# Two places in VectorE's instruction order and the form of one small addition, in an attention and two-stage expert kernel

## The chip, the cores and the metric

The kernel runs on one core of a Trainium2 chip. The metric is device time in microseconds (us) of one execution. The engines are named as in the profile: PE (TensorE, the matrix engine; PEld is its weight load), DVE (VectorE), ACT (ScalarE), POOL (GpSimd) and SP (SyncE, which issues most DMAs). Each engine runs its own instructions strictly in the order in which the program issues them, and waits for other engines through semaphores.

## The reference

Three parts are computed one after the other.

```python
# 1. a linear recurrence per batch (4) and head (8), 768 steps, head size 48
S = a_t * S + k_t v_t^T          # a_t complex, magnitude clipped at 0.999
y_t = q_t Re(S)
x = y as 3072 rows of 384
# 2. experts, stage one: 8 experts, each row goes to the one with the largest logit
e = argmax(x @ w_gate);  g = softmax(...)[e]
x1 = g * (relu(x @ w1[e]) @ w2[e])        # 384 -> 1024 -> 384
# 3. the same again on x1, with 8 other experts and a bias on the logits
#    that one of two modality labels of the row selects
```

## The kernel before, in words

The recurrence is done in 12 units of 2 x 128 time steps, as matrix products on PE with elementwise work on DVE, ACT and POOL. Each step of a unit has a name and a place in a table (`AT`), and the places are sorted into one written-out order for all engines.

Rows are sorted by expert into tiles of 128 rows, padded so that a tile holds rows of one expert. The sorting is prepared while the recurrence still runs. `Router.batch` takes the logits of `n` blocks of 128 rows, makes the one-hot choice `oh` on DVE, and ranks each row within its expert with a few small matmuls on PE into the PSUM tile `pr` (L470 to L473). The last of these reads `acc`, a 128 x 8 bf16 tile with the counts so far. Then DVE sums the choices of this batch into `su` (L475, 128 x 8 f32), adds them to `acc` (L476), and reads `pr` (L478). In the recurrence `pr` lies in a PSUM buffer that later transposes of the recurrence (L339) use again. There are five such batches for stage one (tile `r1acc`) and six for stage two (`r2acc`), the latter during the tiles of stage one.

Each expert stage runs over its tiles in `Stage.run`. A tile's work is a set of named steps, each with a place between about -2 and 10 in the table `POS[stage]`, and `Stage.tile` sorts them by place. For the four quarters q of the hidden layer the steps are: `g1_q` (18 matmuls on PE, L825 to L827), `hh_q` (ACT, relu to f16, L829), `hl_q` (DVE, the remainder that f16 leaves out, L830), and `g2_q` (6 matmuls on PE, L836 to L838, of which the third reads `hl_q`). Other steps prepare coming rows: `sq` (ACT, L775) and `sv` (DVE, four instructions, L777 to L780) scale the rows of tile j+2, and `T`, `xh`, `xl` transpose those of tile j+1 (L790, L794, L796). `ev` (DVE, L842) and `yo` (ACT, L845, and a scatter by POOL, L846) end a tile. In stage one `sv` stands at 6.511 and `ev` at 7.217.

Weights come in f32 and are split into two f16 parts, in eight pieces: `W.split` does the high part `hmq` on ACT (L748) and the low part `lmq` on DVE (L749), with m=0 for the first layer and 1 for the second and q the quarter. These steps stand in `CHG[stage]` with places from 1 to 13.5; a place of 10 or more means the next tile. Each is inside a branch (L861) that is taken when the next tile has another expert. Several tiles of stage one do it; in stage two the changes of expert are at other tiles, among them the last but one. `LATE` gives other places for the tiles from number 23 on, in both stages.

Steps from outside a stage are put in by the table `EXT`: 26.94 means place 6.94 in tile 2. `gate1` is the last part of stage one's gate weights (its fourth step is the DVE instructions L555 to L564).

## Time and profile before

| what | value |
|---|---|
| time, median of 3 runs (lowest to highest) | 782.65 us (781.81 to 783.91) |
| the profiled execution: its own time, and the span of its instructions | 784.11 us, 782.4 us |
| busy share of the span: PE, PEld, DVE, ACT, POOL | 93%, 75%, 68%, 60%, 37% |
| mean granted clock of PE, of full speed | 0.981 |

The recurrence takes roughly the first 270 us, stage one of the experts goes on to about 556 us, and stage two to the end. All rows below are of the profiled execution; its time lies 1.5 us above the median, so a difference worked out in it is taken to the median.

### The profile page before, as it was taken

Reading aid. Unit: us, or ns where it says so; the run is one execution under the profiler, and the core shown is the slowest. Engines: PE = TensorE matmul, PEld = TensorE weight load, DVE = VectorE, ACT = ScalarE, POOL = GpSimd, SP = SyncE. Lnnn points to the kernel's source line nnn. Section 1 sums busy time; section 2 is a strip of 40 time slices with the busy share of each in tenths; the row PEclk is TensorE's granted clock in tenths of the full one; section 3 lists DMA queues with packets and bytes.
Section 4 is the critical chain, followed back from the end, with each engine's and each line's share of the span. In section 5 each row is a group of like instructions: output and inputs, shape, how many; then the busy total and the mean of one; then the engine's idle time right before and its main releaser. Section 6 shows DMA issues by size and latency. Waiting matters only on the chain. (4 is left out here: it accounts for less than half of the span.)

```text
span 782.4 us, 23426 instructions
## 1 busy us (share of the span) xinstructions
PE 730.3 (93%) x8451; PEld 584.0 (75%) x8451; DVE 532.9 (68%) x1415; ACT 470.1 (60%) x1007; POOL 293.1 (37%) x289
## 2 busy tenths in 40 slices
PE   6688999899899989999999998999999999999995
PEld 2467877778788967878777877788777877887873
DVE  7987998898788968474747485855674345545346
ACT  7899989798687336464646464764623335433344
POOL 5657778577575231213122224123121322322221
PEclk9899999899899999999999999999999999999999
DMA  9999777685331342443525152326025111611110
GB/s 220 223 149 220 163 159 165 123 164 96 69 70 62 120 146 94 140 134 114 160 87 175 62 196 78 119 103 204 19 59 188 52 53 44 216 49 43 57 49 30
DMA packets 159260, 91.40 MB, mean 117 GB/s; under 512 B 131804, under 2 KB 149764, under 8 KB 159104
## 3 DMA queue, kind: packets, MB, share of 16 engines
q1 hardware_dynamic: 151872, 68.49, 34.5%
q0 software_dynamic: 7232, 21.05, 8.7%
q8 instruction: 71, 1.16, 0.6%
q14 instruction: 85, 0.70, 0.3%
HBM read 192.54 MB, written 20.84 MB: 273 GB/s over the span
## 5 line engine op out<-in xcount | busy, mean ns | idle before, releaser
L825 PEld LDWEIGHTS <-wh 128*128 128x128 f16 x1296 | 127.3, 98 | 10.9 <-ACTq L891 3.0
L826 PEld LDWEIGHTS <-wh 128*128 128x128 f16 x1296 | 127.3, 98 | 7.3 <-issue 0.5
L827 PEld LDWEIGHTS <-wl 128*128 128x128 f16 x1296 | 127.3, 98 | 0.0
L846 POOL DMA_INDIRECT x<-yo,r1ids x27 | 28.4, 1052 | 191.7 <-ACT hh L829 81.0
L749 DVE SCALAR_TENSOR_TENSOR wl<-ws,wh 128x768 f16<-128x768 f32 x88 | 83.8, 962 | 14.2 <-ACT wh L748 6.7
L748 ACT ACTIVATE wh<-ws 128x768 f16<-128x768 f32 x88 | 74.4, 851 | 10.0 <-ACTq L861 4.8
L838 PEld LDWEIGHTS <-hl 128*128 128x128 f16 x432 | 42.2, 98 | 44.9 <-DVE hl L830 9.5
L838 PE MATMUL mpy<-wh,hl 128*128 128x384 f16 x216 | 70.6, 327 | 3.5 <-DVE hl L830 1.3
L838 PE MATMUL mpu<-wh,hl 128*128 128x384 f16 x216 | 70.5, 327 | 2.7 <-DVE ev L842 1.1
L836 PE MATMUL mpu<-wh,hh 128*128 128x384 f16 x216 | 70.5, 326 | 0.7 <-ACT hh L829 0.6
L836 PE MATMUL mpy<-wh,hh 128*128 128x384 f16 x216 | 70.5, 326 | 0.0
L837 PE MATMUL mpy<-wl,hh 128*128 128x384 f16 x216 | 70.4, 326 | 0.0
L837 PE MATMUL mpu<-wl,hh 128*128 128x384 f16 x216 | 70.4, 326 | 0.0
L846 POOL DMA_INDIRECT out_dram<-yo,r2ids x21 | 21.0, 1002 | 130.1 <-ACT yo L845 115.9
L825 PE MATMUL msc<-xh,wh 128*128 128x128 f16 x384 | 68.5, 221 | 0.9 <-ACTq L891 0.9
L825 PE MATMUL mpk<-xh,wh 128*128 128x128 f16 x384 | 68.0, 220 | 1.3 <-ACTq L891 1.3
L826 PE MATMUL msc<-xl,wh 128*128 128x128 f16 x384 | 68.4, 220 | 0.0
L827 PE MATMUL msc<-xh,wl 128*128 128x128 f16 x384 | 68.4, 220 | 0.0
L830 DVE SCALAR_TENSOR_TENSOR hl<-mpq,hh 128x256 f16<-128x256 f32 x73 | 30.9, 423 | 54.7 <-ACTq L861 21.8
L827 PE MATMUL mpk<-xh,wl 128*128 128x128 f16 x384 | 68.1, 220 | 0.0
L826 PE MATMUL mpk<-xl,wh 128*128 128x128 f16 x384 | 68.0, 220 | 0.0
L825 PE MATMUL mpq<-xh,wh 128*128 128x128 f16 x384 | 67.6, 219 | 0.0
(512 smaller groups left out, 2259.8 us busy)
## 6 DMA issues: line engine op xcount, KB each, us to landing
ws<-in_moe_w_dram SPq DMA_DIRECT2D x100, 1536.0 KB
ar<-in_a_re_dram SPq DMA_DIRECT2D x24, 192.0 KB
ai<-in_a_im_dram SPq DMA_DIRECT2D x24, 192.0 KB
k<-in_k_dram SPq DMA_DIRECT2D x24, 192.0 KB
q<-in_q_dram SPq DMA_DIRECT2D x24, 192.0 KB
v<-in_v_dram SPq DMA_DIRECT2D x24, 192.0 KB
x<-zero SPq DMA_DIRECT2D x8, 576.0 KB
x<-yt SPq DMA_DIRECT2D x24, 192.0 KB
```

The costliest lines, as they stand in the source:

```text
L748: nc.scalar.activation(H_,S_,AF.Copy,scale=WS,accum_out=s.fl[:,s.n:s.n+1]); s.n+=1
L749: if lo: nc.vector.scalar_tensor_tensor(L_,S_,WS,H_,op0=ALU.mult,op1=ALU.subtract)
L825: nc.tensor.matmul(o,W.h1[:,d,fs],x.h[:,d,:],start=(d==0),stop=False)
L826: nc.tensor.matmul(o,W.h1[:,d,fs],x.l[:,d,:],start=False,stop=False)
L827: nc.tensor.matmul(o,W.l1[:,d,fs],x.h[:,d,:],start=False,stop=(d==ND-1))
L830: def hl(q=q): nc.vector.scalar_tensor_tensor(hs[q][2],hs[q][0][:,:,:P],0.0,hs[q][1],op0=ALU.max,op1=ALU.subtract)
L836: nc.tensor.matmul(o,hh[:,r,:],W.h2[:,f,:],start=(f==0),stop=False)
L837: nc.tensor.matmul(o,hh[:,r,:],W.l2[:,f,:],start=False,stop=False)
L838: nc.tensor.matmul(o,hl[:,r,:],W.h2[:,f,:],start=False,stop=(f==NF-1))
L846: nc.gpsimd.indirect_dma_start(out=s.dst,out_offset=bass.IndirectOffsetOnAxis(ap=R.ids[:,j:j+1] if ids is None else ids(),axis=0),in_=y,in ...
```

## The change

Three things are changed. In stage one, `hl_3` moves from place 6.45 to 6.95, that is from ahead of `sv` (6.511) to behind it, and the last step of `gate1` in tile 2 moves from 6.94 to 7.1, so that it stays behind `hl_3`. In stage two, the special place of `l11` for the tiles from number 23 on (11.5, in the next tile) is gone, and its ordinary place (8.43, in the tile itself) holds. The addition of `su` to `acc` is written as a scalar-tensor-tensor instruction, acc times 1.0 plus su, in place of a tensor-tensor addition.

```diff
-POS=[dict(... ev=7.217,hl_3=6.45,ld=7.7,
+POS=[dict(... ev=7.217,hl_3=6.95,ld=7.7,
-LATE=dict(l11=11.5)
+LATE=[dict(l11=11.5),{}]
-    sc3=[16.942,20.231],gate1=[13.14,22.34,23.74,26.94], ...
+    sc3=[16.942,20.231],gate1=[13.14,22.34,23.74,27.1], ...
         su=T([P,E],"su"); nc.vector.tensor_reduce(out=su,in_=oh.rearrange("p n e -> p e n"),op=ALU.add,axis=AX.X)
-        nc.vector.tensor_add(s.acc,s.acc,su)
+        nc.vector.scalar_tensor_tensor(s.acc,s.acc,1.0,su,op0=ALU.mult,op1=ALU.add)
-        when=lambda i,k: LATE.get(k,s.chg[k]) if i>=NT-1 else s.chg[k]
+        when=lambda i,k: LATE[s.n].get(k,s.chg[k]) if i>=NT-1 else s.chg[k]
```

## Rows read from the trace of the kernel before

**Rows 1.** Windows, stage one: length, PE, PEld, DVE, ACT, POOL busy, PEclk, DMA.
```profile
297.00:556.00 259.00, 250.12 (x2947) 198.99 (x2945) 164.78 (x486) 146.31 (x379) 59.32 (x56) 0.99 0.38 126
```
**Rows 2.** Line 476: durations in ns (min/median/max), first and last start.
```profile
L476 DVE TENSOR_TENSOR r2acc<-r2acc,rtsu x6: 166/168/168, 341.4 to 568.3; 128x8 bf16<-128x8 bf16 x6
L476 DVE TENSOR_TENSOR r1acc<-r1acc,rtsu x5: 168/1498/3620, 135.2 to 273.0; 128x8 bf16<-128x8 bf16 x5
```
**Rows 3.** Timeline of DVE: start, length, instruction, count [idle before, releaser].
```profile
135.25 3.62 DVE L476 TENSOR_TENSOR r1acc<-r1acc,rtsu 128x8 bf16<-128x8 bf16 x1 [0.87 <-PE pr L473]
138.79 0.20 DVE L478 SCALAR_TENSOR_TENSOR rtrk<-pr,r1oh 128x48 f32<-128x48 f32 x1
```
**Rows 4.** Timeline of POOL in the same stretch.
```profile
134.48 0.83 POOL L347 TENSOR_TENSOR st<-st,re 112x384 f32<-112x384 f32 x1
135.27 1.80 POOL L265 TENSOR_TENSOR q<-q,Rb 128x768 f32<-128x768 f32 x1
137.04 1.79 POOL L267 TENSOR_TENSOR k<-k,Ri 128x768 f32<-128x768 f32 x1
```
**Rows 5.** Timeline of PE in the same stretch, and 61 us later.
```profile
139.13 0.60 PE L339 MATMUL pr<-ident,Rb 32*64 32x32 f32 x8 [2.94 <-DVE rtrk L478]
...
141.50 2.08 PE L295 MATMUL psc<-qT,kT 112*128 112x128 f32 x8
...
200.12 0.60 PE L339 MATMUL pr<-ident,Rb 32*64 32x32 f32 x8 [2.95 <-DVE rtrk L478]
```
**Rows 6.** Timeline of ACT in the same stretch.
```profile
140.80 0.58 ACT L168 COPY qT<-pq 112x512 f32<-112x512 f32 x1 [2.55 <-PE pq L287]
```
**Rows 7.** Windows, the stretch after that wait.
```profile
139.10:145.90 6.80, 6.77 (x72) 5.88 (x72) 4.92 (x12) 3.49 (x6) 0.00 (x0) 0.57 0.64 84
```
**Rows 8.** Timeline of DVE at two other places of the recurrence.
```profile
98.01 1.73 DVE L749 SCALAR_TENSOR_TENSOR wl<-ws,wh 128x768 f16<-128x768 f32 x1
...
237.44 1.50 DVE L476 TENSOR_TENSOR r1acc<-r1acc,rtsu 128x8 bf16<-128x8 bf16 x1
```
**Rows 9.** Timeline of POOL at these two places.
```profile
97.10 1.82 POOL L265 TENSOR_TENSOR q<-q,Rb 128x768 f32<-128x768 f32 x1
98.87 2.54 POOL L267 TENSOR_TENSOR k<-k,Ri 128x768 f32<-128x768 f32 x1
...
237.10 1.82 POOL L265 TENSOR_TENSOR q<-q,Rb 128x768 f32<-128x768 f32 x1 [1.75 <-ACT Rb L157]
```
**Rows 10.** Timeline of DVE after the recurrence, an instruction of the new form.
```profile
277.99 0.16 DVE L500 SCALAR_TENSOR_TENSOR rffk<-rfnt,fe 128x8 f32<-128x8 f32 x1
```
**Rows 11.** Timeline of DVE around `hl_3` in five tiles of stage one.
```profile
338.04 0.95 DVE L749 SCALAR_TENSOR_TENSOR wl<-ws,wh 128x768 f16<-128x768 f32 x1
338.91 0.42 DVE L830 SCALAR_TENSOR_TENSOR hl<-msc,hh 128x256 f16<-128x256 f32 x1
339.24 0.15 DVE L777 TENSOR_SCALAR ev<-fln 128x1 int32<-128x1 int32 x1
...
340.14 0.15 DVE L842 TENSOR_TENSOR ev<-ev,r1ab 128x1 f32<-128x1 f32 x1
...
347.81 0.42 DVE L830 SCALAR_TENSOR_TENSOR hl<-mpq,hh 128x256 f16<-128x256 f32 x1 [0.43 <-ACTq L861]
...
366.24 0.42 DVE L830 SCALAR_TENSOR_TENSOR hl<-msc,hh 128x256 f16<-128x256 f32 x1 [1.32 <-ACTq L861]
...
459.57 0.42 DVE L830 SCALAR_TENSOR_TENSOR hl<-mpq,hh 128x256 f16<-128x256 f32 x1 [0.43 <-ACTq L861]
...
525.30 0.42 DVE L830 SCALAR_TENSOR_TENSOR hl<-mpq,hh 128x256 f16<-128x256 f32 x1
```
**Rows 12.** Timeline of PE: its matmul on `hl_3`, and one on `hl_0` a tile later.
```profile
339.38 0.34 PE L838 MATMUL mpu<-wh,hl 128*128 128x384 f16 x1 [0.24 <-DVE ev L777]
...
381.34 0.34 PE L838 MATMUL mpy<-wh,hl 128*128 128x384 f16 x1 [0.49 <-DVE hl L830]
```
**Rows 13.** Timeline of DVE at stage two's last change of expert.
```profile
767.32 1.95 DVE L749 SCALAR_TENSOR_TENSOR wl<-ws,wh 128x768 f16<-128x768 f32 x2
```

## The prediction, made before the changed kernel was run

> **What bounds the kernel now.** I read the view of stretches first, then the views of single lines and the timelines. In stage one of the experts PE is busy 250.1 of 259.0 us, while DVE and ACT are busy 165 and 146 [rows 1]. There a step of DVE costs time only where PE waits for it, and where PE has no time left over such a wait passes on in full. In the recurrence the view of line 476 shows something odd: the tiny addition takes 0.17 us in all six batches of stage two, but up to 3.62 us in those of stage one [rows 2]. [...] The addition ends with two POOL instructions that began after it, L265 and L267 [rows 3, 4]. PE sits idle 2.94 us until DVE has read `pr`, which comes right behind the addition, and the same happens 61 us later, to within 0.01 us [rows 5]. [...]

> **The addition in the new form.** Work and operands stay: two inputs and one output in SBUF, 128 x 8. Undisturbed, an instruction of the new form takes 0.16 us against 0.17 [rows 2, 10]; over eleven batches that is nothing. All that matters is whether POOL holds the new form as it held the old. The rows say that it can. A scalar-tensor-tensor instruction with two SBUF inputs at 98.01 took 1.73 us where its like takes 0.95 [rows 8, 11]; it ended at 99.74, 0.82 us behind the end of POOL's L265 at 98.92, and L267 then took 2.54 us in place of 1.79 [rows 4, 9]. So this form too waits for a POOL instruction that is already running, and gets in ahead of the next one. The third slow addition, at 237.44, also waited for one POOL instruction alone, up to 238.92 [rows 8, 9]. The addition at 135.25 and its twin 61 us later are different: they waited through two POOL instructions. The first began 0.02 us ahead of L265, while POOL's L347, on 112 partitions, was about to end at 135.31 [rows 3, 4]. I see no row that says whether this comes from POOL's three instructions in a row or from the form of DVE's instruction. The arrival and POOL's sequence are the same in the new kernel, since nothing ahead of it changes, and the one other trait, two inputs in SBUF, is kept. I take the cost as unchanged: 3.62 us, gain nothing. The other end is 0.16 us.

> What the other end is worth: the idle time of 2.94 and 2.95 us, and the clock, 6.8 x (1 - 0.57) = 2.9 us each, together at most 11.7 us. Already entering between L265 and L267 would let DVE read `pr` at 137.1 in place of 138.8, and PE's idle time would be 1.2 us. The next that would be late is ACT: its copy `qT` waited 2.55 us for PE, so it can't come more than 2.55 us earlier [rows 6], and PE's L295 at 141.50 needs it. With 2.55 us and about half of the clock's 2.9 us, I put it at 4 us for each of the two, 8 in all, whether the addition waits for one POOL instruction or none. By the idle time of the second POOL instruction alone it would be 3.5.

> [...]

> **`hl_3` behind `sv`.** In stage one `sv` takes 0.90 us of DVE, from L777 at 339.24 to the next step's start at 340.14 [rows 11]. Its input, `sq`, stands ahead of `hh_3` on ACT, so `sv` is never the later of the two to be ready, and the order swap holds `hl_3` back by 0.90 us less the time that DVE would have sat idle in front of it. Queued behind `hl_3` is nothing that PE needs sooner. There are three kinds among the 27 tiles.
> Five tiles, the first at 338.91 and the last at 525.30, have no idle time: there `hl_3` follows a split directly, and the full 0.90 us is added [rows 11]. In these PE is already waiting for `hl_3` (0.24 us idle at 339.38 [rows 12]), so all of it reaches PE: 5 x 0.90 = 4.5 us. Part comes back. In the next tile PE waited again, for `hl_0` behind DVE's splits, up to 0.49 us [rows 12]; DVE's total work is unchanged, so a later PE waits less there. I take 0.4 in four of the five: 1.6 us back.
> Four tiles, the first at 347.81 and the last at 459.57, have 0.43 us of idle time, so `hl_3` comes 0.47 later [rows 11]. PE has some room there; I take 0.2 of it, between nothing and 0.47: 0.8 us.
> In the rest, as at 366.24 with 1.32 us idle [rows 11], `sv` fits in ahead, and `hl_3` is not late or PE has room. Here DVE comes free up to 0.9 us sooner, which may spare PE some waits of the following tile: I take 0.5 us in all.
> Sum: 4.5 - 1.6 + 0.8 - 0.5 = 3.2 us slower. The ends: nothing, if later waits give everything back, and 4.5 + 4 x 0.47 = 6.4 if none does. Moving `gate1` only keeps it behind `hl_3`; `sv` and `hl_3` change places there too, and the gate's instructions start at the same time. No DMA and no step of POOL or SP is moved.

> **`l11` in stage two.** The place 8.43 differs from 11.5 only from tile 23 on. In this run one change of expert falls there. DVE did the splits `l03` and `l11` back to back from 767.32 to 769.27 [rows 13]; with the new place they change order and keep the sum. Cover for `l03`, now 0.95 us later, is that `hl_0` stands behind both and `g1_3`, its user, stands two steps further on. One branch more is read in the last tile, within 0.1 us. I take zero.

> **The sum.** Profiled execution: 784.1 + 3.2 = 787.3 us. That execution lies 1.5 above the median; at the median 782.65 + 3.2 = 785.9 us. The bound for faster or slower is 0.3%, 2.35 us, about what a measurement can tell from no change.

> **The rivals.**
> *The addition gets in.* The new form is let in ahead of L267, or at once. For it: of the operations that waited here, both of the shown others waited for one POOL instruction only, and a start some nanoseconds off would already be another race. Against it: the same arrival and the same three POOL instructions. From about 1.6 us per batch it outweighs `hl_3`; at 8 us, 782.65 - 8 + 3.2 = 777.9, faster.
> *The order costs little.* PE's later waits and the earlier `sv` give most of the 4.5 us back, and the addition stays: 0 to 2.3 us, 782.7 to 785.0, no change. For it speaks that PE waits for DVE at several places a tile later; against it, that PE is 97% busy and each of these waits is below half a microsecond.
> *The order costs all.* 6.4 us: 789.1.

> **Chances.** The addition stays and the order costs 2.4 to 5 us: 0.35, the likeliest. The addition stays and the order costs under 2.35 us: 0.25. The order costs more than 5 us: 0.08. The addition gets in: 0.32, of which 0.27 is beyond the bound on the faster side and 0.05 inside it. So faster 0.27, same 0.30, slower 0.43. The likeliest case alone runs from 785 to 787.7. The range that leaves out 2 in 10 takes in most of the first rival (777.9, with the ends 3.5 and 11.7 for its gain it spreads from 774 to 782) and most of the last: 776.5 to 788.5 us.

> **What would show it.** The view of line 476: if the r1 additions still show a maximum near 3.6 us and PE's idle time in front of L339 stays 2.9 us at 139 and 200 us, the first step holds; durations of 0.2 or 1.8 us there, and no stretch at 0.57 of the clock, show the rival. In stage one, the five tiles should show L777 ahead of `hl_3`, and idle time of PE and its weight load in front of L838 larger by 0.9 us; the next tile's wait for `hl_0` should shrink. Stage one should be 3 us longer from 297 us to its end and stage two as long as before. Wrong I'd be if the addition's wait depends on its form, or if DVE has other slack in these five tiles that the timeline hides.

## The result and the profile after

The changed kernel takes 788.77 us (median of 6 runs, 787.87 to 789.31), beside 783.76 us for six runs of the kernel before. The ratio is 1.0066, with a 95% interval of 1.0052 to 1.0080: slower, by some 5 us. The profiled execution took 789.19 us, with a span of 787.5 us. The direction was forecast, though for another step than the one that did it; the size, 785.9 us, was not, and the range ended 0.3 us too low.

First the addition. The view of line 476 of the kernel after, its timelines of DVE and PE, and the stretch behind the wait (columns as in [rows 1]):

```profile
L476 DVE SCALAR_TENSOR_TENSOR r1acc<-r1acc,rtsu x5: 167/1496/3610, 136.5 to 274.4; 128x8 bf16<-128x8 bf16 x5
```
```profile
136.46 3.61 DVE L476 SCALAR_TENSOR_TENSOR r1acc<-r1acc,rtsu 128x8 bf16<-128x8 bf16 x1 [0.86 <-PE pr L473]
139.99 0.19 DVE L478 SCALAR_TENSOR_TENSOR rtrk<-pr,r1oh 128x48 f32<-128x48 f32 x1
```
```profile
140.33 0.60 PE L339 MATMUL pr<-ident,Rb 32*64 32x32 f32 x8 [2.94 <-DVE rtrk L478]
...
201.45 0.60 PE L339 MATMUL pr<-ident,Rb 32*64 32x32 f32 x8 [2.94 <-DVE rtrk L478]
```
```profile
140.30:147.10 6.80, 6.77 (x70) 5.95 (x72) 4.92 (x12) 3.49 (x6) 0.00 (x0) 0.54 0.63 83
```

Nothing changed here. The operation has another name and still lasts 3.61 us, PE sits idle for the same 2.94 us at both places, and the granted clock behind it is 0.54 where it was 0.57 [rows 2, 3, 5, 7].

Then the order in stage one: DVE's and PE's timelines of the kernel after at the tile that [rows 11] begin with.

```profile
339.55 0.95 DVE L749 SCALAR_TENSOR_TENSOR wl<-ws,wh 128x768 f16<-128x768 f32 x1
340.42 0.15 DVE L777 TENSOR_SCALAR ev<-fln 128x1 int32<-128x1 int32 x1
...
341.32 0.42 DVE L830 SCALAR_TENSOR_TENSOR hl<-msc,hh 128x256 f16<-128x256 f32 x1
```
```profile
341.80 0.34 PE L838 MATMUL mpu<-wh,hl 128*128 128x384 f16 x1 [1.14 <-DVE ev L842]
```

`sv` now stands ahead of `hl_3`, 0.90 us from L777 to L830, and PE's wait is 1.14 us where it was 0.24 [rows 12]: the step of 0.90 us, just as forecast. What it does to the whole stage is seen in PE's waits, summed over stage one without the wait at its very end. First the kernel before, then after (line, what it waited for, us in all, times, longest).

```profile
PE mpL L790 <- DVEq L861: 2.0, 1, 2.0
...
PE mpy L838 <- DVE hl L830: 1.3, 3, 0.5
PE mpu L838 <- DVE ev L777: 0.9, 4, 0.2
PE mpt L1173 <- ACT yo L845: 0.9, 2, 0.6
PE mpt L573 <- DVE guess L629: 0.6, 1, 0.6
PE mpy L838 <- issue: 0.6, 3, 0.2
PE mpu L836 <- ACT hh L829: 0.6, 1, 0.6
PE mpu L838 <- DVEq L861: 0.3, 1, 0.3
PE mpT L608 <- DVE r2eAQ L604: 0.3, 1, 0.3
```
```profile
PE mpu L838 <- DVE ev L842: 4.9, 6, 1.1
PE mpL L790 <- DVEq L861: 2.1, 1, 2.1
PE mpy L838 <- DVE ev L842: 1.0, 2, 0.8
PE mpy L838 <- DVE hl L830: 0.8, 2, 0.4
PE mpu L838 <- DVE hl L830: 0.4, 1, 0.4
PE mpu L838 <- DVEq L861: 0.3, 1, 0.3
PE mpt L1173 <- ACT yo L845: 0.2, 1, 0.2
```

The waits in front of L838 grow from 3.1 to 7.4 us in sum. But four other waits that PE had a little later (L1173, L573, L836, L608, together 2.4 us) shrink to 0.2: PE arrives there later and no longer waits. From one and the same L825 matmul near the start of stage one to the first L825 of stage two it is 269.98 us before (285.78 to 555.76) and 270.31 after (287.14 to 557.45). So 0.3 us are left in this pair, not 3.2. These two stretches, before and then after (columns as in [rows 1]):

```profile
285.78:555.76 269.98, 259.15 (x3050) 206.11 (x3048) 172.53 (x516) 152.25 (x394) 61.99 (x59) 0.99 0.37 124
287.14:557.45 270.31, 257.61 (x3050) 206.65 (x3047) 173.27 (x516) 154.01 (x394) 64.77 (x59) 0.99 0.38 124
```

The four waits give back 2.2 of the 4.3 us. Most of the rest is PE's busy time, 1.5 us less for the same 3050 matmuls, and no step is known for that. One pair can't settle so small a cost either. In e1, e3 and e4 below, with the old order, the same stretch takes 270.3 to 271.0 us; in e2, with the new one, 272.3, in the slowest of its twelve executions. In two other series it is 263.6 with the new order (e9) and 263.7 to 264.8 with the old (e10 to e12), then 270.4 (e15) and 268.2 to 269.5 (e13, e14, e16). So the difference lies between -1.1 and 2.2 us, everywhere below 3.2.

The bulk is at the end. DVE's and PE's timelines, before and then after:

```profile
778.01 0.19 DVE L1305 TENSOR_SCALAR_CACHE_REDUCE ckb<-fly 128x31 f32<-128x31 f32 x1 [1.57 <-DVEq L917]
...
778.52 0.38 PE L1308 MATMUL mpT<-ckout,ckon 128*128 128x1 f32 x2 [3.10 <-DVE ckout L1274]
```
```profile
768.86 1.82 DVE L749 SCALAR_TENSOR_TENSOR wl<-ws,wh 128x768 f16<-128x768 f32 x2
...
777.39 0.42 DVE L780 TENSOR_SCALAR xs<-xg,ev 128x384 f32<-128x384 f32 x1
783.19 0.18 DVE L1305 TENSOR_SCALAR_CACHE_REDUCE ckb<-fly 128x31 f32<-128x31 f32 x1 [5.37 <-DVEq L917]
...
783.63 0.59 PE L1308 MATMUL mpT<-ckout,ckon 128*128 128x1 f32 x2 [6.83 <-DVE ckout L1274]
```

L917 is the branch past the tiles that this input doesn't need; L1305 is the first instruction behind it. DVE sits idle there for 5.37 us in place of 1.57. The views of the branches' lines show where (operation, count, durations in ns, first and last start). L917 stands for two jumps here, the taken branch and, behind two semaphore instructions at its target, a jump out. Before, then after, and last L861, the branches around the splits, after:

```profile
L917 DVEq COMPARE_BRANCH  x2: 79/102/124, 776.6 to 777.5; - x2
L917 DVEq EVENT_SEMAPHORE  x2: 21/21/21, 777.3 to 777.5; - x2
```
```profile
L917 DVEq COMPARE_BRANCH  x2: 75/104/133, 778.7 to 782.8; - x2
L917 DVEq EVENT_SEMAPHORE  x2: 21/21/21, 782.6 to 782.7; - x2
...
L861 DVEq COMPARE_BRANCH  x2: 114/114/114, 777.4 to 778.0; - x2
```

From the end of the taken branch to the first instruction at its target it is 0.63 us before and 3.75 after: 3.1 of the 3.8 us more. The other 0.7 are the L861 at 778.0, a branch that the kernel before doesn't have at this place. From the split at the last change of expert (768.86; 767.32 in [rows 13]) to L1305 it is 14.33 us after and 10.69 before: 3.64 us more. Of the 5.18 us by which L1305 comes later, 1.36 were there when stage one began (287.14 against 285.78), 0.33 come from stage one, -0.15 from stage two up to that split, and 3.64 from the last 15 us. I put the 1.36 us down to the execution: e1 to e4 below, of which only e1 differs from the kernel before ahead of stage one, enter it at 286.21, 286.46, 284.86 and 284.35.

### The profile page after: what moved, and what is told of

Its sections match the earlier page's. It is cut to its first block, busy times and chain, and to the rows that moved or that the text cites. A ratio compares the mean times of both kernels' runs of the same rounds, so it can differ in the third digit from the quotient of the medians.

```text
span 787.5 us, 23428 instructions
## 1 busy us (share of the span) xinstructions
PE 732.0 (93%) x8451; PEld 586.4 (74%) x8451; DVE 533.2 (68%) x1415; ACT 471.9 (60%) x1007; POOL 295.6 (38%) x289
## 5 line engine op out<-in xcount | busy, mean ns | idle before, releaser
L825 PEld LDWEIGHTS <-wh 128*128 128x128 f16 x1296 | 127.2, 98 | 10.8 <-ACTq L891 3.0
L846 POOL DMA_INDIRECT x<-yo,r1ids x27 | 30.7, 1138 | 189.2 <-ACT yo L845 114.6
L838 PEld LDWEIGHTS <-hl 128*128 128x128 f16 x432 | 42.2, 98 | 47.1 <-DVE hl L830 16.1
L838 PE MATMUL mpu<-wh,hl 128*128 128x384 f16 x216 | 70.6, 327 | 7.0 <-DVE ev L842 6.0
L838 PE MATMUL mpy<-wh,hl 128*128 128x384 f16 x216 | 70.5, 327 | 3.3 <-DVE ev L842 1.7
L836 PE MATMUL mpu<-wh,hh 128*128 128x384 f16 x216 | 70.7, 327 | 0.0
L836 PE MATMUL mpy<-wh,hh 128*128 128x384 f16 x216 | 70.5, 326 | 0.0
L825 PE MATMUL msc<-xh,wh 128*128 128x128 f16 x384 | 68.5, 221 | 0.9 <-ACTq L891 0.9
L825 PE MATMUL mpk<-xh,wh 128*128 128x128 f16 x384 | 67.6, 219 | 1.3 <-ACTq L891 1.3
L826 PE MATMUL mpq<-xl,wh 128*128 128x128 f16 x384 | 67.6, 219 | 0.0
L827 PE MATMUL mpq<-xh,wl 128*128 128x128 f16 x384 | 67.6, 219 | 0.0
```

The source lines that it names most:

```text
L825: nc.tensor.matmul(o,W.h1[:,d,fs],x.h[:,d,:],start=(d==0),stop=False)
L826: nc.tensor.matmul(o,W.h1[:,d,fs],x.l[:,d,:],start=False,stop=False)
L827: nc.tensor.matmul(o,W.l1[:,d,fs],x.h[:,d,:],start=False,stop=(d==ND-1))
L836: nc.tensor.matmul(o,hh[:,r,:],W.h2[:,f,:],start=(f==0),stop=False)
L838: nc.tensor.matmul(o,hl[:,r,:],W.h2[:,f,:],start=False,stop=(f==NF-1))
L846: nc.gpsimd.indirect_dma_start(out=s.dst,out_offset=bass.IndirectOffsetOnAxis(ap=R.ids[:,j:j+1] if ids is None else ids(),axis=0),in_=y,in ...
```

## The experiments

All times are compared with runs of the kernel before on the same chip in the same series; the series differ (776.4 to 786.2 us for the kernel before). e5, e6, e7, e10, e14 and e16 were executed once each and give no ratio. Idle times are those of one profiled execution.

**The three parts alone.** Each keeps the other parts as before; the fourth run splits `l11` from the branch that goes with it.

```diff
# e1
+        nc.vector.scalar_tensor_tensor(s.acc,s.acc,1.0,su,op0=ALU.mult,op1=ALU.add)
# e2
+... hl_3=6.95 ...  gate1=[13.14,22.34,23.74,27.1]
# e3
+LATE=[dict(l11=11.5),{}]
# e4
-        when=lambda i,k: LATE.get(k,s.chg[k]) if i>=NT-1 else s.chg[k]
+        when=lambda i,k: LATE.get(k,s.chg[k]) if i>=NT-1+s.n else s.chg[k]
```

> The kernel before with the addition alone in the new form. Theory (as predicted): the form changes nothing, the r1 additions still last up to 3.6 us, and the time is within 0.3 us of the kernel before. Rival: the form matters somewhere that the maximum does not show, and the time moves by 1 us or more either way.

> The kernel before with hl_3 behind sv, and the gate's last step behind it, alone. Theory from the two traces: PE's waits for hl_3 grow by 6 us in sum, but 2.5 us come back at hl_0 and hl_1 and more at a step that is not tied to DVE, so 0.4 to 1.2 us slower. The prediction: 3.2 us slower. Rival, that the order is the whole cause: 5 us slower.

> The kernel before with l11 of stage two at its ordinary place alone. Theory: DVE's branch behind the last tile takes some 3 us longer (3.8 in place of 0.6 us to its next instruction), all of it on the path that ends last, so 3.5 us slower. The prediction, and the rival that the end of the trace was an accident of one execution: 0 us.

> The kernel before with l11 at 8.43 in tile 23 of stage two and at 11.5 from tile 24 on, so that the change of expert is split in the new order, while the last tile has no branch for l11 at 8.43. Theory, that the additional branch between the prefetch hint and the last branch is the cause: no loss, within 0.3 us of the kernel before. Rival, that the order of l11 and l03 at the change of expert is the cause: 3.5 us slower.

| run | ratio to before (95%) | idle before L1305 |
|---|---|---|
| e1, addition | 0.9991 (0.9971 to 1.0012) | 1.57 us |
| e2, `hl_3` | 0.9999 (0.9981 to 1.0017) | 1.57 us |
| e3, `l11` | 1.0042 (1.0022 to 1.0062) | 5.19 us |
| e4, `l11` in tile 23 alone | 0.9997 (0.9978 to 1.0016) | 1.57 us |

Only `l11` costs time: 3.3 us of 786.22 (1.7 to 4.9). `hl_3` costs between -1.5 and 1.3 us; the forecast's 3.2 is outside. In e4 the change of expert is split in the new order, and nothing is lost. So it is not the order of the splits, but what the new place does to the last tile.

**What loses the time at the branch.** In the last tile that is worked on (24), the changed kernel has a branch for `l11` at 8.43 that the kernel before doesn't have there. Its body is not run. (The one that belongs to tile 23 has left the start of tile 24, place 1.5, for tile 23 itself.) Is it the branch itself, what stands between the hint and L917, or the place of L917 in DVE's program?

```diff
# e5 (tile 24, place 8.43); e6: the same at place 0.5
+    with s.tc.If(chg[1]!=0): s.tc.nc.vector.memset(s.W.scr,0.0)
# e7 (tile 24, place 8.43)
+    for _ in range(4): s.tc.nc.vector.memset(s.W.scr,0.0)
# e8, on the changed kernel, stage two
-    mid.append((HINT, ...        # 1.5
+    mid.append((5.0, ...
```

> The kernel before with one more branch on DVE in the last tile of stage two (place 8.43, behind the prefetch hint at 1.5), on the same condition as l11; its body is one memset of a spare column and is not run. Theory, that what stands between the hint and the last branch decides: the idle time before DVE's L1305 is 5 us or more, as in the changed kernel, in place of 1.6. Rival, that only the moved split does it: 1.6 us.

> The same additional branch in the same tile at place 0.5, ahead of the hint. Everything behind it lies as many instructions further on as in the run before. Theory, that what stands between the hint and the branch decides: idle time 1.6 us before L1305. Rival, that the address of the last branch in the program decides: 5 us or more.

> The kernel before with four memsets of a spare column, without a branch, at place 8.43 of the last tile: the same number of instructions as the branch of the other two runs. If the number of branches that DVE takes behind the hint decides: idle time 1.6 us before L1305. If the number of instructions behind the hint, or the address, decides: 5 us or more.

> The changed kernel with stage two's hint for the skipped tiles at place 5 in place of 1.5, on all five engines. Theory, that the hinted code is lost by what DVE does between hint and branch: with three splits fewer in between the idle time before L1305 is back at 1.6 us and the time 3.5 us below the changed kernel, at that of the kernel before. [...]

DVE's timeline behind the branch in e6 and e7 (L1309 is L1305, L921 is L917, moved by the added lines):

```profile
774.64 0.18 DVE L1309 TENSOR_SCALAR_CACHE_REDUCE ckb<-fly 128x31 f32<-128x31 f32 x1 [4.68 <-DVEq L921]
```
```profile
775.18 0.18 DVE L1309 TENSOR_SCALAR_CACHE_REDUCE ckb<-fly 128x31 f32<-128x31 f32 x1 [5.31 <-DVEq L921]
```

e5 shows 5.43 us. The theory on record fell: a branch ahead of the hint loses nearly as much (4.68 us idle) as one behind it, and four plain memsets do so too (5.31). The later hint in e8 gave 4.04 us and a ratio of 1.0056 (1.0037 to 1.0076): the idle time lies between the 1.57 of the kernel before and the 5.37 of the kernel after, but no time is saved. e8 also changed more than meant. The tile has a second hint, at place 4, for the next branch (L1250), and the moved hint now stands behind it. From L1250 to the first instruction at its target DVE takes 3.9 us in e8, and 0.5 in the kernels before and after, so the 1.2 us won at L917 were lost again there. What e5, e6 and e7 share is that L917 stands four or five instructions further on.

**The place of the branch.** Blocks of memsets of a spare column, inside a branch that always skips them, move everything behind.

```diff
# tile 20, 120 (e9, on the changed kernel), 30 (e10), 113 (e14)
# tiles 19 and 21, 118 each (e13), 115 each (e15, on the changed kernel), 95 each (e16)
+    with s.tc.If(s.regs(NT)[1]!=0):
+        for _ in range(120): s.tc.nc.vector.memset(s.W.scr,0.0)
```

> The changed kernel with a block of 120 memsets of a spare column in tile 20 of stage two, inside a branch that is always taken past them, so that they lie in DVE's program but are not run. Everything behind lies some 120 instructions further on; the order of the steps is that of the changed kernel. Theory, that the place of the last branch in the program decides (four instructions more lost the hint in three runs, wherever they stood): the idle time before DVE's L1305 falls from 5.4 to about 1.6 us, and the time is 3.5 us below the changed kernel, within 0.3% of the kernel before. Rival, that any lengthening of the program in front of the branch loses it: 5 us idle, 0.5% slower than the kernel before.

> The kernel before with the same block at the same place, of 30 memsets. Theory, that the place decides and that a few instructions more than in the kernel before is a bad place: 5 us idle before L1305. Rival, that the skipped block itself repairs it (which would also explain the other run): 1.6 us.

> The kernel before with two blocks of 118 memsets, skipped by branches that are always taken, in tiles 19 and 21 of stage two: the last branch lies 246 instructions further on in DVE's list. Theory, that the place decides and repeats every 256 instructions (10 fewer kept the hinted code, so 246 more should): 1.6 us idle before L1305, the time of the kernel before. Rival, that any lengthening loses it: 4 us or more idle, and 0.3% to 0.5% slower.

> The kernel before with one such block of 113: the last branch lies 118 further on. If the place repeats every 128 instructions: 1.6 us idle before L1305. If it repeats every 256, or any lengthening loses it: 4 us or more.

> The changed kernel with two such blocks of 115: its last branch lies 246 further on than in the kernel before, as in the first run of this call, with all three edits in place. Theory, that the place repeats every 256 instructions: 1.6 us idle before L1305, and 3.5 us below the changed kernel, so within 0.3% of the kernel before. Rival, that the order of l11 matters beside the place, or that any lengthening loses it: 4 us or more idle.

> The kernel before with two such blocks of 95: the last branch lies 200 further on. If the place repeats every 256 instructions and the good places are those in which hint and branch lie in one stretch of 256: 1.6 us idle before L1305. If the good places are only a few: 4 us or more.

The table sorts all runs by the place of L917 in DVE's list of instructions, counted in the built programs against the kernel before (where the hint stands 71 places ahead of it).

| L917 moved by | runs | idle before the first instruction behind it |
|---|---|---|
| -10, -8 | e11, e12 (below) | 1.55 us each |
| 0 | before, e1, e2, e4 | 1.57 us each |
| +4, +5, +5, +6, +6 | e7, e5, e6, e3, after | 5.31, 5.43, 4.68, 5.19, 5.37 us |
| +6, its hint +30 | e8 | 4.04 us |
| +35 | e10 | 3.77 us |
| +118 | e14 | 3.66 us, of another kind |
| +131 | e9 | 5.49 us |
| +200 | e16 | 1.55 us |
| +246 | e13, e15 | 3.66 us, of another kind; 2.04 us |

The wait alone, from the end of the taken branch to the first instruction at its target, is 0.62 to 0.64 us in the rows with 1.55 to 2.04 us and in those of another kind; it is 2.6 us in e8, 2.9 in e10 and 3.6 to 3.9 in the other late ones. In e3 and the kernel after, the code behind the branch hasn't moved, since a skipped tile has one branch less; so the place of the target alone doesn't decide.

More code ahead doesn't lose the time by itself: 200 instructions more lose nothing, and in e15, with all three edits in place, 2.04 us are left (the 0.5 above 1.55 is the additional branch) and the ratio is 1.0005 (0.9986 to 1.0025): no cost of the changed kernel is left that a measurement can tell, once its last branch stands elsewhere. e9, the first attempt at that, missed (1.0038, 1.0024 to 1.0053): 131 is a bad place again. e13 shows a second kind, in the chain that ended last (start, length, what):

```profile
777.90 0.08 DVEq L927
777.98 2.38 issue
780.36 0.02 DVEq L1315
```

L927 is L917 there. The branch itself is past in time, but 2.38 us go by "issue" behind the second jump of this line, where the kernel before shows 0.29. The run is slower too, 1.0030 (1.0013 to 1.0047): its expectation was missed, though the branch itself behaved. e14 shows the same 3.66 us, put down to "issue".

**What the held addition costs.** The rival of 8 us was not tried by the change, as the addition stayed held. Two kernels let PE go: e11 moves the addition behind the reads of `pr`, e12 in addition puts `su` into PSUM.

```diff
# both, on the kernel before: behind L479 in place of ahead of L478
-        su=T([P,E],"su"); nc.vector.tensor_reduce(out=su, ...)   # e12; e11 leaves it
-        nc.vector.tensor_add(s.acc,s.acc,su)
         rk=...; r=...
+        su=pr[:,64:64+E]; nc.vector.tensor_reduce(out=su, ...)   # e12
+        nc.vector.tensor_add(s.acc,s.acc,su)
```

> The kernel before with the addition behind the two instructions that read the ranks, L478 and L479, so that PE's buffer comes free before DVE is held. Theory (the rival of the prediction, whose price this measures): PE's 2.94 us in front of L339 shrink to 0.2 us at both places. But DVE is still held for about 3.4 us, and its copy kT, which PE's L295 needs, comes only 0.3 us earlier, so the gain is small: 0 to 2 us. The prediction's price for a free PE was 8 us.

> The same late place, and the sum su lies in PSUM, in free columns of the ranks' tile, so that the addition has one input in SBUF and one in PSUM. Theory, that POOL holds DVE's instructions with two inputs in SBUF: the r1 additions last 0.2 us each, DVE goes on at once, kT comes 3 us earlier, and the time falls by 4 to 8 us. Rival, that POOL holds it for another reason: the maximum stays above 3 us and the time moves by less than 2 us.

e11: 0.9955 (0.9937 to 0.9974), 3.5 us faster (2.0 to 4.9). e12: 0.9858 (0.9833 to 0.9884), 11.0 us of 776.43 (9.0 to 13.0; the medians lie 10.0 apart), the fastest kernel here. Timelines of DVE, POOL and PE, first e11, then e12, and the windows of e12 at both places, with that of the kernel before at the first:

```profile
135.26 1.81 POOL L265 TENSOR_TENSOR q<-q,Rb 128x768 f32<-128x768 f32 x1
137.04 1.80 POOL L267 TENSOR_TENSOR k<-k,Ri 128x768 f32<-128x768 f32 x1
...
135.60 3.27 DVE L479 TENSOR_TENSOR r1acc<-r1acc,rtsu 128x8 bf16<-128x8 bf16 x1
138.79 0.68 DVE L169 COPY kT<-pk 112x512 f32<-112x512 f32 x1
...
140.12 1.52 PE L295 MATMUL psc<-qT,kT 112*128 112x128 f32 x8 [2.50 <-DVE A L298]
```
```profile
135.50 1.81 POOL L265 TENSOR_TENSOR q<-q,Rb 128x768 f32<-128x768 f32 x1
...
136.22 0.16 DVE L479 TENSOR_TENSOR r1acc<-r1acc,pr 128x8 bf16<-128x8 bf16 x1
136.30 0.68 DVE L169 COPY kT<-pk 112x512 f32<-112x512 f32 x1
...
137.95 1.16 PE L295 MATMUL psc<-qT,kT 112*128 112x128 f32 x8
```
```profile
135.00:146.00 11.00, 10.70 (x135) 8.83 (x133) 10.34 (x20) 10.41 (x15) 8.24 (x6) 1.00 0.84 151
196.00:207.00 11.00, 10.62 (x105) 8.48 (x106) 10.57 (x17) 9.76 (x17) 10.31 (x8) 1.00 0.30 74
```
```profile
135.00:146.00 11.00, 8.05 (x88) 6.88 (x84) 8.84 (x14) 6.81 (x10) 3.89 (x4) 0.69 0.82 126
```

In e11 PE's wait for `pr` is gone (2.94 us before, none in front of L339 at 136.11), and 2.50 us come back two steps on: DVE is still held, so `kT` and the scores behind it are late. That is the wait the expectation named, and it still left 3.5 us, more than the 2 expected. The addition began 0.34 us behind L265 here and was held through L267 too, so to arrive just ahead of a POOL instruction is not what makes it wait through two. In e12 the addition runs 0.16 us while POOL's L265 is at work, `kT` comes 2.49 us earlier than in e11, and the granted clock of these 11 us is 1.00, where the kernel before has 0.69. The gain lies in the recurrence: stage one's L825 from above comes at 273.65 us in e12 and at 285.61 in e10, which has the recurrence of the kernel before on the same chip.

## Why the prediction was wrong

**The addition: right.** It was said that POOL can hold the new form as it held the old, and that the maximum, PE's 2.94 us and the low clock stay. All three did, and e1 alone is within 0.3% of before. The rival that it gets in didn't happen. Its price was probably too low: 8 us were forecast, 11.0 (9.0 to 13.0) measured with e12, in which no r1 addition is held. e12 also moves the addition behind the reads of `pr`, so it is the nearest price on record and not the rival itself. The cap of 2.55 us, taken from ACT's wait for `qT`, doesn't hold there: PE's L295 began 6.23 us behind POOL's L265 before [rows 4, 5] and 2.45 us behind it in e12, 3.8 us earlier. The sentence that the new form "gets in ahead of the next one" was read from a single split at 98.01 us. It is no rule for such additions: the one in e11, in the old form, arrived under L265 as well and did not get in ahead of L267.

**`hl_3`: the mechanism right, one term mis-sized.** The gross term, 4.5 + 0.8 = 5.3 us, is near the 4.3 us by which the waits at L838 grew. "I take 0.4 in four of the five: 1.6 us back" was the mis-sized one: 0.3 us are left in the profiled pair, and e2 allows no more than 1.3. I had looked for the return only at the next waits for `hl_0`. What can be seen of it, 2.2 us, came at waits for ACT and for the routing's small steps, which have nothing to do with `hl_3`; where the rest came back is open. The rival "the order costs little" had the size right.

**`l11`: the step that failed.** "One branch more is read in the last tile, within 0.1 us. I take zero." e3 puts the measured price at 3.3 us (1.7 to 4.9), 3.6 in the profiled pair. No row stood behind the 0.1 us. DVE's branch records of L861 last 0.04 to 0.15 us in the kernel before, but the additional branch as a whole takes 0.5 us in e15 and 0.7 in the kernel after. The larger part, 3.1 us, I had not thought of: the branch's instructions move another branch, on the path that ends last, to a place from which its target's first instruction starts 3.75 us behind it and not 0.63. So the kernel became slower, as forecast, by a step that was taken at zero, while the step that was to cost 3.2 us shows no cost in e2: the direction was luck. "The order costs all" gave 789.1 us and is near the result by accident too; its cause was not what happened.

The parts alone add up to 2.5 us, -0.7 - 0.1 + 3.3, and the whole measured 5.0; each has an uncertainty of some 1.5 us, so this is no contradiction, but nothing finer than that is settled.

**What stays open.** That the place of the branch decides is shown by the table; why is not. All rows fit a border that recurs every 128 instructions and lies within three of the old place of L917, behind it. It then falls between hint and branch in each bad run (+4 to +35, and 131 = 128 + 3); in the others it lies behind the branch (-10, -8, 0, 118 = 128 - 10, 246 = 256 - 10) or about at the hint (200 = 128 + 72, the hint 71 ahead). These counts are of the built program; the compiler drops jumps to the very next instruction. In the compiled one L917 stands at -10, -8, +4, +5, +34, +117, +129, +198, +243 and +244, the hint 58 ahead; the same border then lies directly behind the old place, and in e16 11 instructions ahead of the hint. That is a reading of eleven places, its period found after the fact, and no run shows what such a border is. The second kind, behind the branch at +118 and +246, is open as well.

## What to carry to other kernels

Where a chain ends behind a taken branch, read the idle time of the first instruction behind it in every version: an edit that adds nothing but a few unexecuted instructions ahead can cost microseconds there (3.3 in e3), and moving the code by a skipped block tells such a cost from the edit's own. When an engine with slack is made to do two steps in another order, look for the return at all later waits of the engine that waits for it, whoever these are for: here 2.2 of 4.3 us came back at four waits for other steps. A tiny instruction that lasts microseconds is worth more than its own length: here 2.94 us of PE's wait and a clock of 0.57 came with 3.62 us, and with one operand in PSUM it was 0.16 us and a clock of 1.00.

## What the runs showed of the hardware

**One operand in PSUM.** The same addition, while the same POOL instruction runs, took 3.27 us with both inputs in SBUF (e11) and 0.16 us with one of them in PSUM (e12). With both in SBUF it ended within 0.04 us of the end of POOL's L267 (at 138.87 us, L267 at 138.83 [rows 3, 4]; 138.87 and 138.84 in e11); with one in PSUM it ended at 136.38, while L265 ran to 137.31. Why it was held through two POOL instructions and not one, whether it arrived 0.02 us ahead of the first [rows 3, 4] or 0.34 us behind its start (e11), stays unexplained.
